# A jump over unused TensorE code, and fifteen tiny loads, in a decode attention kernel

## The chip, the core and the metric

The kernel runs on one core of a Trainium2 chip. A core has five engines with programs of their own: TensorE (PE: matrix products into PSUM; the profile keeps its weight loads apart as PEld), VectorE (DVE), ScalarE (ACT), GpSimd (POOL) and SyncE (SP), which here only issues transfers. [...] Engines wait for each other by semaphores. The metric is the device time of one execution in microseconds; lower is better.

## The reference

One decode step for a batch of two: attention over a cache of 4096 keys with 16 query heads on 8 key-value heads of width 256, gated by a small feed-forward network. All is float32.

```python
xn = layernorm(x)                       # x: (2, 1, 448)
q = xn @ wq                             # 16 heads of 256
p = softmax(q @ k_cache^T * 256**-0.5)  # k_cache, v_cache: (2, 8, 4096, 256)
s = (p @ v_cache) @ wo                  # back to 448
h = (xn @ w_gate) * (xn @ w_up)         # 1792 wide
g = silu(h @ w_down)
out = x + s * g
```

The caches are 134 MB of the 158.5 MB that are read, and each byte is used once.

## The kernel before, in words

`N = 16` units of work, one for each pair of a key-value head and a batch row. A unit needs 4 MB of keys and 4 MB of values. The host lays the data out so that one transfer of 8 MB (`kv[1 + i]`, line 172) brings the keys of unit i+2 beside the values of unit i. Two buffers of 64 KB on each of 128 partitions (`buf[0]`, `buf[1]`) take these transfers in turn; `low` holds the gate, up and later the output weights.

**SyncE's queue** (`dma_side`, lines 160 to 185) sets the order of all large loads: gate and up weights in two pieces (line 163), `wz`, a strip of the up weights, from four rows of HBM to sixteen partitions (line 164), `wd` (165), `wq` (166). Then, each behind a wait for the product that frees its buffer: the first unit's and the second's keys (169), fourteen transfers of 8 MB (172), the last two units' values (175), the output weights in six pieces (180), the result (182). Each load counts 16 on a semaphore when it has landed. ScalarE issues two small loads of x at its start (223, 225).

**TensorE** (`pe_side`, line 358) runs one program in order: transposes of the normalised x; gate and up products (403) once `gu` is full; the feed-forward's down product (409, key "y4") and its sums (412); q's products (415) and their transposes (418, key "qt"). Then for units 0 and 1 `scores`, `highest` and `spread_highest` (lines 463 to 467), with `turn(0)` between, and a loop of `LOOPS = 7` turns (line 471) with two units each: `turn` transposes the exponentials, `scores` is the next keys' product, `values` the product with the values, `join` collects heads. Behind the loop come the last two units and the output weights (495 to 511). `scores` first waits for `q`, which GpSimd counts up when a unit's q is laid out (line 219), and for the keys' load.

`Queue.after` (line 50) makes one engine wait for a numbered point of another's program; `Queue.loop` (line 70) opens a loop on the hardware and passes further arguments on to `nc.Fori`. [...] VectorE and ScalarE run their own loops, with softmax's maxima, exponentials and sums, paced by TensorE.

Of the kernel before, what the change touches and what calls it, by code (L numbers as in the profile page):

```python
# [5 lines left out]
PE = mybir.EngineType.PE  # L6
# [18 lines left out]
EPS = 1e-5  # L25
N = HKV * B
LOOPS = 7
SIDE = 256
GU = (0, 2 * FC, 28 * FC - SIDE)
GROUPS = 4  # L30
# [59 lines left out]
def program(nc, known, x, xo, wgu, wz, wd, wq, kv, vv, wo, out):  # L90
    def flat(w, lo, hi):
        return w[128 * lo:128 * hi].rearrange("(p n) -> p n", p=128)

    def sb(name, shape):
        return nc.alloc_sbuf_tensor(name, shape, F32).ap()

    def ps(name, shape):
        return nc.alloc_psum_tensor(name, shape, F32).ap()

    first = nc.alloc_semaphore("first")  # L100
    sems = {n: nc.alloc_semaphore(n) for n in (
        "x", "xg", "gu", "wd", "wq", "k0", "k1", "v14", "v15", "t0", "t1", "pt", "sr", "ob", "q", "m", "mx", "res")}
    won = [nc.alloc_semaphore(f"wo{i}") for i in range(len(ABREAST + DIRECT))]
    pe = Queue(nc, nc.tensor, "pe", known)
    dv = Queue(nc, nc.vector, "dv", known)
# [15 lines left out]
    xg, gate, sig, r0, r1 = (sb(n, [128, SL]) for n in ("xg", "gate", "sig", "r0", "r1"))  # L121
# [8 lines left out]
    m = sb("m", [128, 2])  # L130
    mx = sb("mx", [1, NT, W])
    p = sb("p", [128, 2, 512])
    su = sb("su", [128, 2])
    sr = sb("sr", [128, 128])
    r = sb("r", [128, N, REP])
    pT = sb("pT", [128, 2, BLK, 128])
    ob = sb("ob", [128, 512])
    oT = sb("oT", [128, REP, 2, N, DUP])

    s = ps("s", [128, 2, 512])  # L140
    sm = ps("sm", [128, 512])
    pt = [ps(f"pt{i}", [128, NK, 128]) for i in range(2)]
# [4 lines left out]
    late = buf[1][:, ROW:]  # L147
    side = late[:4 * GROUPS, :8 * SIDE]
    bounds = [0]
# [10 lines left out]
    def dma_side():  # L160
        e = nc.sync
        for lo, hi in zip(GU, GU[1:]):
            e.dma_start(low[:, lo:hi], flat(wgu, lo, hi)).then_inc(sems["gu"], 16)
        e.dma_start(side, wz[:, :4]).then_inc(sems["gu"], 16)
        e.dma_start(buf[1][:, :14 * D], wd).then_inc(sems["wd"], 16)
        e.dma_start(buf[0][:, :28 * 512], wq).then_inc(sems["wq"], 16)
        sp.after(pe, "y4")
        for h in range(2):
            e.dma_start(buf[1][:, h * ROW:(h + 1) * ROW], kv[0][:, h * ROW:(h + 1) * ROW]).then_inc(sems[f"k{h}"], 16)
        for i in range(N - 2):  # L170
            sp.after(pe, *(("q", 1) if i == 0 else ("s", 1) if i == 1 else ("v", i - 2)))
            e.dma_start(buf[i % 2], kv[1 + i]).then_inc(turns[i % 2], 16)
        sp.after(pe, "v", N - 4)
        for h in range(2):
            e.dma_start(buf[0][:, h * ROW:(h + 1) * ROW], vv[h]).then_inc(sems[f"v{N - 2 + h}"], 16)
        for n, lo, hi in zip(won, bounds, bounds[1:]):
            if lo == early:
                sp.after(pe, "v", N - 3)
            t = low[:, lo * D:hi * D] if hi <= early else late[:, (lo - early) * D:(hi - early) * D]
            e.dma_start(t, flat(wo, lo * D, hi * D), single_packet=True).then_inc(n, 16)  # L180
        sp.after(dv, "res")
        e.dma_start(out, r1).then_inc(sems["res"], 16)
        e.wait_ge(sems["res"], 16)
        last = nc.alloc_semaphore("last")
        e.sem_clear(range(first.num, last.num + 1))

# [171 lines left out]
    def pe_side():  # L358
        e = nc.tensor

        def rows(t, w, n, cut=0):
            def block(i):
                return w[:, i * n:(i + 1) * n - (cut if i == 13 else 0)]
            for k in range(3):
                for c in range(NT):
                    e.matmul(t[W * c:W * (c + 1), :n], xnT[:, k, :], block(NT * k + c), start=k == 0, stop=False)  # L366
            if cut:
                z = side.rearrange("p (a k n) -> p a k n", a=2, k=NK)
                for k in range(NK):
                    for c in (1, 3):  # L370
                        e.matmul(t[W * c:W * (c + 1), n - cut:n], xzT[:, k, :], z[:, c // 2, k, :],
                                 start=False, stop=False)
            for c in range(NT):
                half = slice(0, 64) if c < 2 else slice(64, 128)
                ins = e.matmul(t[W * c:W * (c + 1), :n - cut * (c % 2)], xnT[half, 3, :], block(12 + c % 2)[half],
                               start=False, stop=True)
            return ins
# [24 lines left out]
        for w in range(2):  # L402
            pe.ev(rows(s[:, w], low[:, w * 14 * FC:(w + 1) * 14 * FC], FC, w * SIDE), "gu", w)
        pe.after(dv, "h")
# [15 lines left out]
        def scores(i, k):  # L420
            pe.take(sems["q"])
            k = k.rearrange("p (h d c n) -> p h d c n", h=2, d=2, c=NT)
            for h in range(2):
                for d in range(2):
                    for c in range(NT):
                        ins = e.matmul(s[W * c:W * (c + 1), h], qs[i % 2][:, d].rearrange("p j q -> p (j q)"),  # L426
                                       k[:, h, d, c, :], start=d == 0, stop=d == 1)
            pe.ev(ins, "s", i)

        def highest(i):  # L430
            pe.take(sems["m"])
            pe.ev(e.transpose(sm[:1, :128], m[:, 0:1], ident), "m", i)  # L432

        def spread_highest(i):
            pe.take(sems["mx"])
            pe.ev(e.matmul(sm[:, 128:129], mx.rearrange("p c j -> p (c j)"), one, start=True, stop=True), "x", i)  # L436

        def turn(i):
            pe.take(sems["sr"])
            for h in range(2):  # L440
                pe.ev(turned(pt[h], p[:, h]), "t", i, h)
            pe.ev(e.matmul(sm[:, 130:132], sr, sel[:, 0], start=True, stop=True), "u", i)  # L442

        def values(i, v, between):
            v = v.rearrange("p (h i c n) -> p h i c n", h=2, i=BLK, c=2)
            for h in range(2):
                for j in range(BLK):
                    between.get((h, j), lambda: None)()
                    for c in range(2):
                        at = 2 * (j % 2) + c  # L450
                        ins = e.matmul(o[W * at:W * (at + 1), :], pT[:, h, j, 64 * c + 16:64 * c + 48],  # L451
                                       v[:, h, j, c, :], start=h == 0 and j < 2, stop=h == 1 and j >= 2)
            pe.ev(ins, "v", i)

        def join(i):
            pe.take(sems["ob"])
            for d in range(2):
                for h in range(2):
                    ins = e.matmul(oc[:, 2 * d:2 * d + 2], ob[:, h * 256 + d * 128:h * 256 + (d + 1) * 128], sel[:, h],  # L459
                                   start=h == 0, stop=h == 1)  # L460
            pe.ev(ins, "j", i)

        for i in range(2):
            e.wait_ge(sems[f"k{i}"], 16)
            scores(i, buf[1][:, i * ROW:(i + 1) * ROW])
            highest(i)
            spread_highest(i)
            if i == 0:
                turn(0)

        with pe.loop(nc, PE, LOOPS, head_slot={PE: 0}):
            for i in range(2):
                pe.take(sems["pt"], 2)
                turn(i + 1)
                pe.take(turns[i], 16)
                scores(i + 2, buf[i][:, ROW:])
                values(i, buf[i][:, :ROW], {(0, 3): lambda: highest(i + 2), (1, 2): lambda: spread_highest(i + 2)})
                join(i)
# [35 lines left out]
    act_side()  # L514
    dve_side()
    dma_side()
    pe_side()
    return {q.name: q.at for q in (pe, dv, ac, po, sp)}

# [53 lines left out]
```

## Time and profile before

| | |
|---|---|
| device time, median of 3 runs | 374.89 us (374.56 to 375.03) |
| device time of the profiled execution | 374.87 us |
| its span in the profile | 373.1 us |
| bytes moved, mean rate over the span | 158.68 MB, 425 GB/s |
| TensorE matmul busy, mean granted clock | 247.5 us (66%), 0.799 |
| VectorE, ScalarE, GpSimd busy | 58.4 us, 46.5 us, 5.9 us |

The page gives for each engine its busy time; a strip of digits for forty equal slices of the span (9 means 90% or more); the DMA queues with their packets, MB and share of the time of all sixteen DMA engines; and the chain of work that ended last. Queue q1 is SyncE's, q10 ScalarE's, q8 carries blocks of TensorE's program. A view by stretches cuts the span at chosen times and gives for each stretch the length, the busy time and number of instructions of each engine, the granted clock, the share of the sixteen DMA engines that was busy, and GB/s. The view of the DMA queues can be cut to a stretch as well; its shares then are of sixteen engines over that stretch.

### The profile page before, as it was taken

How to read it: one execution, taken by the hardware profiler on the slowest of the kernel's cores; microseconds unless marked ns; L12 is line 12 of the kernel's file. 1: busy time of each engine (PE TensorE's matmuls, PEld its weight loads, DVE VectorE, ACT ScalarE, POOL GpSimd, SP SyncE). 2: the span in 40 equal slices, each digit the busy share in tenths (PEclk: the TensorE clock that was granted, in tenths of full speed). 3: DMA queues.
4: the chain of work that ended last, by engine and by line, in shares of the span. 5: the costliest groups of instructions: out<-in, count | busy, mean ns of one | idle time of the engine just before them, and what ended most of it. 6: DMA issues, size and time to landing. Idle time of an engine off the chain costs nothing. (4 is left out here: it accounts for less than half of the span.)

```text
span 373.1 us, 3992 instructions
## 1 busy us (share of the span) xinstructions
PE 247.5 (66%) x1662; PEld 100.2 (27%) x1662; DVE 58.4 (16%) x132; ACT 46.5 (12%) x111; POOL 5.9 (2%) x30
## 2 busy tenths in 40 slices
PE   0097485539393949585767767576857585948785
PEld 0022123122223232323232314132222323232432
DVE  3001003202121212121120212030303020202100
ACT  1000231200201020202020202020202020112100
POOL 2000000000000000000000000000000000000000
PEclk9996699858786776877685968595969595869899
DMA  9999999999999999999999999999999999999995
GB/s 363 407 460 450 405 436 425 451 444 422 436 444 429 414 450 443 414 436 450 429 414 450 443 414 436 450 429 414 450 443 414 436 443 422 429 422 436 415 418 229
DMA packets 4221, 158.68 MB, mean 425 GB/s; under 512 B 614, under 2 KB 872, under 8 KB 1256
## 3 DMA queue, kind: packets, MB, share of 16 engines
q1 hardware_dynamic: 4196, 158.59, 98.6%
q8 instruction: 5, 0.08, 0.1%
q10 hardware_dynamic: 20, 0.01, 0.0%
HBM read 158.54 MB, written 0.06 MB: 425 GB/s over the span
## 5 line engine op out<-in xcount | busy, mean ns | idle before, releaser
L426 PE MATMUL s<-buf,qs 128*32 128x512 f32 x512 | 85.9, 831 | 53.2 <-PEq L87 53.2
L451 PE MATMUL o<-buf,pT 128*32 128x512 f32 x512 | 76.0, 602 | 0.3 <-DVE oT L328 0.3
L246 ACT ACTIVATE p<-s,m 128x512 f32<-128x512 f32 x32 | 21.7, 682 | 250.7 <-DVE m L310 250.7
L426 PEld LDWEIGHTS s<-buf,qs 128*32 128x32 f32 x512 | 21.8, 147 | 104.2 <-issue 104.2
L304 DVE TENSOR_REDUCE m<-s 128x1 f32<-128x1024 f32 x16 | 19.6, 1225 | 167.8 <-PE s L426 167.8
L381 PE MATMUL pt<-ident,p 128*128 128x128 f32 x128 | 26.1, 372 | 17.9 <-PEq L87 17.9
L459 PE MATMUL oc<-sel,ob 128*128 128x2 f32 x128 | 16.4, 250 | 19.8 <-PEq L87 19.8
L381 PEld LDWEIGHTS pt<-ident,p 128*128 128x128 f32 x128 | 20.4, 188 | 18.8 <-issue 18.8
L451 PEld LDWEIGHTS o<-buf,pT 128*32 128x32 f32 x512 | 16.9, 110 | 31.5 <-issue 29.1
L459 PEld LDWEIGHTS oc<-sel,ob 128*128 128x128 f32 x128 | 15.5, 191 | 33.9 <-issue 33.9
L366 PE MATMUL s<-low,xnT 128*32 128x448 f32 x48 | 6.9, 725 | 12.4 <-DMA buf<-wz 12.4
L323 DVE COPY pT<-pt 128x512 f32<-128x512 f32 x16 | 11.1, 692 | 19.6 <-PE o L451 18.5
L306 DVE TENSOR_REDUCE mx<-sm 1x128 f32<-1x512 f32 x16 | 10.9, 679 | 10.1 <-PE sm L432 10.1
L258 ACT COPY ob<-o 128x512 f32<-128x512 f32 x16 | 9.3, 582 | 12.6 <-PE o L451 12.6
L366 PE MATMUL s<-buf,xnT 128*32 128x512 f32 x48 | 7.1, 737 | 4.9 <-DMA buf<-wq 4.9
L251 ACT COPY pT<-pt 128x512 f32<-128x512 f32 x16 | 9.6, 601 | 2.3 <-PE pt L381 2.3
L328 DVE TENSOR_TENSOR oT<-oc,r 128x64 f32 (+1 forms) x16 | 3.6, 225 | 32.5 <-PE oc L459 32.5
L442 PEld LDWEIGHTS sm<-sel,sr 128*128 128x128 f32 x32 | 8.6, 330 | 0.0
L436 PEld LDWEIGHTS sm<-one,mx 1*128 1x128 f32 x32 | 4.7, 183 | 13.8 <-issue 13.8
L219 POOL COPY qs<-qT 128x64 f32<-128x64 f32 x16 | 3.7, 237 | 292.6 <-PE s L426 243.1
L386 PE MATMUL o<-low,oT 128*32 128x448 f32 x54 | 6.4, 544 | 1.2 <-DMA low<-wo 1.2
L436 PE MATMUL sm<-one,mx 1*128 1x1 f32 x32 | 6.0, 254 | 1.7 <-PEq L87 1.7
(70 smaller groups left out, 73.6 us busy)
## 6 DMA issues: line engine op xcount, KB each, us to landing
buf<-kv SPq DMA_DIRECT2D x2, 4096.0 KB, 20.3
buf<-vv SPq DMA_DIRECT2D x2, 4096.0 KB, 22.2
buf<-wq SPq DMA_DIRECT2D x1, 7168.0 KB, 40.2
low<-wgu SPq DMA_DIRECT2D x1, 5696.0 KB
buf<-wd SPq DMA_DIRECT2D x1, 3136.0 KB, 23.5
low<-wo SPq DMA_DIRECT2D x1, 3136.0 KB, 33.9
low<-wo SPq DMA_DIRECT2D x1, 2016.0 KB, 38.2
low<-wo SPq DMA_DIRECT2D x1, 896.0 KB, 39.9
```

The source lines that it names most:

```text
L246: ins = e.activation(p[:, h], s[:, h], AF.Exp, bias=m[:, 1:2], scale=1.0 / 16, accum_out=su[:, h:h + 1])
L251: e.copy(pT[:, 1], pt[1]).then_inc(sems["pt"], 1)
L258: e.copy(ob, o).then_inc(sems["ob"], 1)
L304: e.tensor_reduce(m[:, 0:1], s.rearrange("p h n -> p (h n)"), axis=AX.X, op=OP.max).then_inc(sems["m"], 1)
L306: e.tensor_reduce(mx, sm[:1, None, :128].rearrange("p o (c j) -> p o j c", c=NT).to_broadcast([1, NT, W, NT]), axis=AX.X, op=OP.max).then_ ...
L323: e.tensor_copy(pT[:, 0], pt[0]).then_inc(sems["pt"], 1)
L366: e.matmul(t[W * c:W * (c + 1), :n], xnT[:, k, :], block(NT * k + c), start=k == 0, stop=False)
L381: ins = e.transpose(t[:, i, :], a[:, i * 128:(i + 1) * 128], ident)
L426: ins = e.matmul(s[W * c:W * (c + 1), h], qs[i % 2][:, d].rearrange("p j q -> p (j q)"), k[:, h, d, c, :], start=d == 0, stop=d == 1)
L436: pe.ev(e.matmul(sm[:, 128:129], mx.rearrange("p c j -> p (c j)"), one, start=True, stop=True), "x", i)
L451: ins = e.matmul(o[W * at:W * (at + 1), :], pT[:, h, j, 64 * c + 16:64 * c + 48], v[:, h, j, c, :], start=h == 0 and j < 2, stop=h == 1 an ...
L459: ins = e.matmul(oc[:, 2 * d:2 * d + 2], ob[:, h * 256 + d * 128:h * 256 + (d + 1) * 128], sel[:, h], start=h == 0, stop=h == 1)
```

## The change

Three things change. SyncE gets fifteen loads between `wd` and `wq`: the load of k rows (k = 1 to 15) brings k rows of 16 numbers of x, 64 bytes a row, to k partitions of a new tensor `lab`. Nothing reads `lab`; at the end SyncE waits for all fifteen. TensorE gets, behind q's transposes, a register that holds 0 and a branch on it: the code that would run if it weren't 0 is 1,720 waits, and it is always passed over. And TensorE's loop loses its `head_slot`.

```diff
+FILL = 1720
...
-        "x", "xg", "gu", "wd", "wq", "k0", "k1", "v14", "v15", "t0", "t1", "pt", "sr", "ob", "q", "m", "mx", "res")}
+        "x", "xg", "gu", "wd", "wq", "k0", "k1", "v14", "v15", "t0", "t1", "pt", "sr", "ob", "q", "m", "mx", "lab", "res")}
...
+    lab = sb("lab", [16, 240])
+    xr = x.rearrange("b (k n) -> (b k) n", n=16)
...
         e.dma_start(buf[1][:, :14 * D], wd).then_inc(sems["wd"], 16)
+        for k in range(1, 16):
+            e.dma_start(lab[:k, (k - 1) * 16:k * 16], xr[:k]).then_inc(sems["lab"], 16)
         e.dma_start(buf[0][:, :28 * 512], wq).then_inc(sems["wq"], 16)
...
         e.wait_ge(sems["res"], 16)
+        e.wait_ge(sems["lab"], 15 * 16)
...
+        never = e.alloc_register("never")
+        e.reg_mov(never, 0)
+        with e.If_ne(never, 0):
+            for _ in range(FILL):
+                e.wait_ge(sems["gu"], 16)
+
         for i in range(2):
             e.wait_ge(sems[f"k{i}"], 16)
             scores(i, buf[1][:, i * ROW:(i + 1) * ROW])
...
-        with pe.loop(nc, PE, LOOPS, head_slot={PE: 0}):
+        with pe.loop(nc, PE, LOOPS):
```

The change's own description says that TensorE's program "jumps to its sixth block".

## The prediction

> **What bounds the kernel now.** I read the strip of forty slices first, then the table of DMA queues, then the chain that ended last.
>
> ```profile
> PE   0097485539393949585767767576857585948785
> DMA  9999999999999999999999999999999999999995
> DMA packets 4221, 158.68 MB, mean 425 GB/s; under 512 B 614, under 2 KB 872, under 8 KB 1256
> q1 hardware_dynamic: 4196, 158.59, 98.6%
> q8 instruction: 5, 0.08, 0.1%
> DMA 7%; PE 3%; DVE 0%; issue 0%
> ```
>
> The 16 DMA engines are busy in every slice; SyncE's queue alone (q1) fills 98.6% of their time. TensorE idles between loads. The chain is short because it starts at the last weight loads, which had been queued long before. The span is the time in which 16 engines move 158.68 MB, and as all feed every transfer, the end is that of the engine with the most to carry. So I ask of each edit which DMA engine it loads. The second queue that matters is q8: five packets of 0.08 MB in all, 16 KB each, TensorE's own program.
>
> ```profile
> core 0: us, PE busy (x) PEld busy (x) DVE busy (x) ACT busy (x) POOL busy (x), PEclk, DMA share, GB/s
> 368.00:368.20 0.20, 0.20 (x8) 0.00 (x0) 0.00 (x0) 0.00 (x0) 0.00 (x0) 1.00 0.96 367
> 368.20:368.60 0.40, 0.40 (x7) 0.00 (x0) 0.00 (x0) 0.00 (x0) 0.00 (x0) 1.00 0.71 269
> 368.60:369.30 0.70, 0.04 (x1) 0.00 (x0) 0.00 (x0) 0.53 (x1) 0.00 (x0) 1.00 0.58 220
> 369.70:369.90 0.20, 0.20 (x16) 0.20 (x12) 0.00 (x0) 0.00 (x0) 0.00 (x0) 1.00 0.14 54
> 369.90:370.10 0.20, 0.20 (x18) 0.20 (x13) 0.00 (x0) 0.00 (x0) 0.00 (x0) 1.00 0.01 0
> buf<-wz SPq DMA_DIRECT2D x1, 128.0 KB
> ```
>
> These stretches show the engines running dry. The share is 0.96 until 368.2, falls to 0.58 by 368.6, stays there, and is gone at 369.9. A share of 0.58 is 9.3 engines: seven stop between 368.0 and 368.6, nine go on to between 369.3 and 369.9. I read the nine as five with one program block each and four with `wz`. `wz` is loaded from 4 rows, so I put its 128 KB on four engines: 32 KB at 425 / 16 = 26.6 GB/s, 1.2 us each. 4 + 5 = 9 fits only if no engine carries both; one that did would have run on past 370.4.
>
> **The program blocks.**
>
> ```profile
> 0.00:35.10 35.10, 15.12 (x108) 5.04 (x112) 4.35 (x13) 2.23 (x4) 2.23 (x14) 0.92 0.98 418
> 35.10:67.70 32.60, 21.54 (x157) 7.45 (x153) 3.88 (x11) 6.94 (x15) 0.65 (x3) 0.82 0.98 425
> 67.70:77.50 9.80, 4.88 (x33) 2.84 (x25) 2.36 (x4) 1.45 (x4) 0.24 (x1) 0.82 1.04 450
> 77.50:106.40 28.90, 18.24 (x117) 6.71 (x121) 3.29 (x7) 2.41 (x6) 0.24 (x1) 0.71 0.99 429
> DMA packets 2099, 108.34 MB, mean 432 GB/s; under 512 B 232, under 2 KB 232, under 8 KB 232
> q1 hardware_dynamic: 2099, 108.34, 99.8%
> ```
>
> I cut the stretches at the fetches (35.1, 67.7, 77.6, 106.5, 359.2). The x behind PEld counts weight loads, each with a matmul. By the code 280 pairs stand ahead of the loop, 170 in its body, 192 behind: 280 + 7 x 170 + 192 = 1662, the page's count. The third fetch comes 290 pairs in, ten after the loop's head; the fourth after 131 pairs of the loop, some 270 instructions with its waits. [...] The last two lines are q1 alone from 108 to 359 us: no q8 line, so six back edges fetch nothing.
>
> **The change part by part.**
>
> *The jump.* [...]
>
> ```profile
> PE s L426 <- PEq L87: 6.3, 2, 5.4
> 82.42 1.94 PE L426 MATMUL s<-buf,qs 128*32 128x512 f32 x8 [5.38 <-PEq L87]
> q8 instruction: 1, 0.02, 3.1%
> q8 instruction: 1, 0.02, 3.4%
> 69.87 0.33 SPq L172 DMA_DIRECT2D buf<-kv  x1
> ```
>
> TensorE must wait at the target for block six. The trace of before shows no such wait. Its least is one fetch, 3.1% of 16 engines in two us = 0.99 us (3.4% = 1.09 in the slowest); its most, with two 64 KB packets of 2.4 us ahead on that engine (65,536 B at 26.6 GB/s), 6 us. I take 3. Queued behind it are scores(0), turn(0), scores(1), and SyncE's load of the second block of keys, issued at 69.87 when scores(1) ends. The cover: TensorE sits idle 5.38 us ahead of the scores at 82.42, waiting for a load that ends there, and the queue is full until then, 12 us after 69.87. So the stall costs nothing; six us would pass 0.6 into a loop with 53 us of such idle time. The compare and the register move lie under the same cover.
>
> [...]
>
> *What the blocks do to DMA engines.* A block costs its engine from 0.62 us (16 KB at 26.6 GB/s) to 1.6 us (369.9 less 368.3, the middle of the plain engines' ends). I take 1.3, between the packet's own 1.0 and the 1.6. [...] A plain engine with one block ends where such engines end now. A `wz` engine with a block ends at 369.5 + 1.3.
>
> *Fifteen loads.* [...]
>
> ```profile
> q10 hardware_dynamic: 8, 0.00, 1.8%
> q10 hardware_dynamic: 8, 0.00, 0.6%
> 3.18 0.51 SPq L166 DMA_DIRECT2D buf<-wq  x1
> 1.65 0.79 SPq L164 DMA_DIRECT2D buf<-wz  x1
> buf<-wd SPq DMA_DIRECT2D x1, 3136.0 KB, 23.5
> 371.48 0.35 SPq L182 DMA_DIRECT2D res<-r  x1
> ```
>
> The nearest rows are the eight 448-byte rows of `xg` (1.8% of 16 engines in 0.7 us, 25 ns each) and their eight semaphore writes (0.6%, 8 ns). [...] I take 0.4 on `wz`'s engines. Alone this is hidden: 369.5 + 0.4 is 369.9, the end as it is. On SyncE the loads stand ahead of `wq`, at 0.35 to 0.79 us an issue: `wq`, issued at 3.18 now, goes out between 8.4 and 15.0. `wd` ahead of it lands at about 2.5 + 23.5 = 26, so the queue stays full, and the next issue waits for y4 at 37. The wait at the end is met long before; under 0.1 us.
>
> [...]
>
> **The sum.** The profiled execution took 374.87 us, with a span of 373.1 and 1.8 around it; the runs' median is 374.89. Jump 0, issue 0, small loads 0 by themselves. With block eight, nine or ten on one of `wz`'s engines: 369.5 + 1.3 + 0.4 = 371.2 against 369.9, **+1.3 us, 376.2**. Its ends: 369.3 + 0.6 + 0.1 is 370.0 (+0.1), 369.9 + 1.6 + 0.5 is 372.0 (+2.1); by the prices that I hold likely 375.6 to 376.8. The slip carries to the end in full, as the last products wait for the last weights:
>
> ```profile
> 344.08 25.18 DMA buf<-wo
> 369.30 0.78 PE acc L504 x24
> ```
>
> **The rivals.**
>
> *Not slower: the new blocks miss `wz`'s engines.* [...] From -0.1 to +0.5 us; I take +0.2, **375.1**. For it: five fetches of before all missed. It turns into the forecast once one of two or three blocks meets one of four engines. If engines are given evenly among the eleven left, two blocks miss with 7/11 x 6/10 = 0.38, three with 0.21. [...]
>
> [...]
>
> *The change doesn't do what it says:* the fill is laid elsewhere, or the same engines carry as many blocks. Then the small loads alone, 0 to +0.3, **375.0**.
>
> *Faster* by more than 0.2%: four engines of `wz` end no sooner than 369.3, 0.6 us ahead of now, whatever the blocks do. Hardly.
>
> **How the numbers follow.** Forecast 0.56; miss 0.32; blocks don't stay 0.05; not as said 0.07. About 0.2%, 0.75 us, is what a measurement here can tell. Slower by more: 0.52 of the forecast's 0.56 (the rest ends under +0.75), 0.05, and 0.02 of a miss: 0.59. Faster 0.03, from a miss with cheaper engines than I think. Same 0.38. The range runs from 374.6 (a miss, less 0.2 and the runs' spread) to 377.0 (+2.1); it leaves out the store that loses blocks and the far tails. The likeliest case alone: 375.6 to 376.8.
>
> **What would show it.** q8 with five or six packets: one at 35 as now, two close together at 52 to 60, one in the loop's first turns, none later, one or two near 358. TensorE's first scores later than 54.73 by 1 to 6 us, those at 82.42 unmoved. In the last two us one or two engines still running from 370.1 to 371.3, where before had none: this decides between forecast and miss. I am wrong if the share falls to zero by 370.2; if the tail is long for many engines, the small loads cost more than 33 ns; if q8 has 20 packets, blocks don't stay.

## The result and the profile after

The changed kernel takes 377.28 us (median of 5 runs, 376.26 to 377.58) against 374.81 for the kernel before in the same comparison (374.56 to 375.03): ratio 1.0058, interval 1.0040 to 1.0077. That is 2.47 us more. The forecast was 376.2 in a range of 374.6 to 377.0: slower was right, the size was too small by half and the median lies 0.28 us above the range. The profiled execution took 377.52 us with a span of 376.0.

First the strip of GB/s on the page of the kernel before, and then, from the page of the changed kernel, the same strip, the packets, and the program's queue.

```profile
GB/s 363 407 460 450 405 436 425 451 444 422 436 444 429 414 450 443 414 436 450 429 414 450 443 414 436 450 429 414 450 443 414 436 443 422 429 422 436 415 418 229
```

```profile
GB/s 360 404 409 417 418 436 448 441 376 434 446 446 432 439 418 404 439 446 432 446 441 432 439 418 418 432 446 425 446 446 432 439 418 411 439 425 422 423 421 213
DMA packets 4462, 158.70 MB, mean 422 GB/s; under 512 B 854, under 2 KB 1112, under 8 KB 1496
q8 instruction: 6, 0.10, 0.1%
```

241 packets more than the 4221 of before: 1 + 2 + ... + 15 = 120 rows of 64 bytes, as many semaphore writes, and one program block more. The page agrees: 240 packets more under 512 B (854 against 614), so the rows of these fifteen loads took one packet of data and one semaphore write each. Two places of the strip are low against the kernel before: the third and fourth slice (19 to 38 us, 409 and 417 against 460 and 450) and the ninth (75 to 85 us, 376 against 444). The stretches around them, in the kernel before and then in the changed one:

```profile
22.00:32.00 10.00, 8.22 (x68) 2.51 (x60) 1.31 (x3) 0.79 (x3) 0.00 (x0) 0.88 1.06 460
72.00:96.00 24.00, 14.75 (x87) 6.35 (x87) 3.44 (x7) 3.85 (x10) 0.24 (x1) 0.72 1.01 435
```

```profile
22.00:32.00 10.00, 8.53 (x68) 2.56 (x60) 1.30 (x3) 0.53 (x1) 0.00 (x0) 0.92 1.03 415
72.00:96.00 24.00, 17.39 (x109) 7.65 (x111) 5.47 (x10) 3.48 (x9) 0.47 (x2) 0.73 0.97 413
```

In the first stretch the engines move 415 instead of 460 GB/s: the fifteen loads pass there, with their 64-byte packets from 24.3 to 26.9 us. In the second their share is 0.97 instead of 1.01. A share has to be read with care: a packet is counted in the stretch in which it begins, with all of its time, so a share can pass 1, and one round of sixteen packets of 2.4 us is 0.2 of a stretch of 12 us. Over the 12 us that the expectations below name (78 to 90 us) the shares are 0.92 and 1.01, and the ten kernels that show no hole scatter there from 0.96 to 1.02; over 72 to 96 us they lie between 0.99 and 1.01. Added up from the packets' starts and durations in the traces, sixteen packets are under way at every time from 74 to 92 us in the kernel before, and only about nine at 81 to 82 us in the changed one. That is the hole. What stands around that hole shows in the timeline of the changed kernel, TensorE's lines first and then SyncE's:

```profile
55.37 1.43 PE L387 MATMUL pt<-ident,qr 128*128 128x128 f32 x8
62.91 6.08 PE L432 MATMUL s<-buf,qs 128*32 128x512 f32 x32 [6.11 <-PEq L88]
76.34 4.49 PE L432 MATMUL s<-buf,qs 128*32 128x512 f32 x32
87.99 5.48 PE L432 MATMUL s<-buf,qs 128*32 128x512 f32 x32
8.48 0.39 SPq L171 DMA_DIRECT2D buf<-wq  x1
80.90 0.33 SPq L177 DMA_DIRECT2D buf<-kv  x1
```

q's transposes begin at 55.37 (52.37 before). The jump then leaves TensorE idle for 6.11 us. scores(0) takes 6.08 us instead of 3.64, at a granted clock of 0.59 instead of 1.00, as the stretch of these products shows in the kernel before and in the changed one:

```profile
54.70:58.40 3.70, 3.64 (x32) 1.12 (x32) 0.00 (x0) 0.81 (x1) 0.06 (x1) 1.00 1.03 443
```

```profile
62.90:69.00 6.10, 6.08 (x32) 1.49 (x32) 0.00 (x0) 0.00 (x0) 0.00 (x0) 0.59 1.11 475
```

SyncE's second transfer of 8 MB, which waits for scores(1), is issued at 80.90 instead of 69.87. (The expectations below call it the third unit's keys; "the keys" in what follows is this transfer; by line 172 of the kernel before it brings the fourth unit's keys and the second unit's values.) It is 11.03 us late: 3.00 of late start, 5.18 of stall (62.91 less 54.73, less those 3.00), 2.44 of slow scores, 0.4 of the rest. By then the engines that were ahead had moved all that was queued: of sixteen, ten are at work at 81.0 us and nine from 81.3 to 82.0.

The end of the changed kernel answers to the tail shown in the prediction:

```profile
370.40:370.80 0.40, 0.40 (x5) 0.16 (x8) 0.00 (x0) 0.00 (x0) 0.00 (x0) 1.00 1.00 376
370.80:371.20 0.40, 0.40 (x8) 0.00 (x0) 0.00 (x0) 0.00 (x0) 0.00 (x0) 1.00 0.71 264
371.20:371.60 0.40, 0.28 (x4) 0.00 (x0) 0.00 (x0) 0.05 (x1) 0.00 (x0) 1.00 0.43 166
372.40:372.80 0.40, 0.40 (x28) 0.40 (x24) 0.00 (x0) 0.00 (x0) 0.00 (x0) 1.00 0.11 40
372.80:373.20 0.40, 0.40 (x24) 0.29 (x14) 0.00 (x0) 0.00 (x0) 0.00 (x0) 1.00 0.00 0
```

All sixteen engines run until 370.8, not until 368.2, and the last stops at about 372.8, not at 369.9. The first to stop slipped by 2.6 us and the last by 2.9. One or two engines that met a program block would have left the first at 368.2: the loss reached every engine of this execution.

### The profile page after: what moved, and what is told of

Read it like the earlier page. It is cut to its first block, busy times and chain, and to the rows that moved or that the text cites. A ratio compares the mean times of both kernels' runs of the same rounds, so it can differ in the third digit from the quotient of the medians.

```text
span 376.0 us, 4009 instructions
## 1 busy us (share of the span) xinstructions
PE 253.9 (68%) x1662; PEld 102.4 (27%) x1662; DVE 58.4 (16%) x132; ACT 46.6 (12%) x111; POOL 6.0 (2%) x30
## 5 line engine op out<-in xcount | busy, mean ns | idle before, releaser
L432 PE MATMUL s<-buf,qs 128*32 128x512 f32 x512 | 91.0, 873 | 49.2 <-PEq L88 49.2
L432 PEld LDWEIGHTS s<-buf,qs 128*32 128x32 f32 x512 | 24.4, 153 | 102.4 <-issue 102.1
L372 PE MATMUL s<-buf,xnT 128*32 128x512 f32 x48 | 8.1, 828 | 6.3 <-DMA buf<-wq 6.3
```

## The experiments

Each was compared with the kernel before on the same chip. Ratios are to the kernel before, with their intervals; its median was 375.02 us for the first four, 374.97 for the next four and 374.9 for the last two.

**The fifteen loads alone.** The change without the jump and with `head_slot` kept; the tensor `lab` and the wait at the end, not printed here, are as in the change:

```diff
         e.dma_start(buf[1][:, :14 * D], wd).then_inc(sems["wd"], 16)
+        for k in range(1, 16):
+            e.dma_start(lab[:k, (k - 1) * 16:k * 16], xr[:k]).then_inc(sems["lab"], 16)
         e.dma_start(buf[0][:, :28 * 512], wq).then_inc(sems["wq"], 16)
```

> Theory A: the small loads, not a meeting of a program block with the wz engines, make the larger part of the loss. In the changed kernel wq lands at 8.48 + 36.8 = 45.3 us against 3.18 + 40.2 = 43.4 before, so the slowest engine is 1.9 us late before any new block has been fetched. Then the loads alone cost +1.4 to +2.2 us (376.2 to 377.0), wq lands at 45 or later, five fetches on q8, and no dip of the DMA share at 78 to 90 us. Theory B, the forecast as it was recorded (a new block on one of wz's engines, loads at 33 ns each): 0 to +0.3 us, wq lands by 43.9.

376.40 us, ratio 1.0034 (1.0022 to 1.0046): +1.4 us. wq lands at 8.50 + 37.4 = 45.9. The stretches of this kernel show the first low group without the second:

```profile
22.00:32.00 10.00, 8.32 (x68) 2.51 (x60) 1.31 (x3) 0.70 (x2) 0.00 (x0) 0.88 0.97 409
78.00:90.00 12.00, 7.20 (x46) 3.69 (x50) 0.24 (x1) 0.00 (x0) 0.00 (x0) 0.60 1.00 433
```

The loads make more than half of the loss by themselves, with five program blocks as before. Theory A holds for them. The end of this kernel's profiled execution (377.20 us, one of the slowest two of six):

```profile
368.20:368.60 0.40, 0.40 (x8) 0.13 (x4) 0.00 (x0) 0.00 (x0) 0.00 (x0) 1.00 0.99 390
368.60:369.00 0.40, 0.40 (x8) 0.13 (x4) 0.00 (x0) 0.00 (x0) 0.00 (x0) 1.00 0.72 291
372.00:372.40 0.40, 0.40 (x24) 0.40 (x20) 0.00 (x0) 0.00 (x0) 0.00 (x0) 1.00 0.07 27
372.40:372.80 0.40, 0.40 (x27) 0.35 (x16) 0.00 (x0) 0.00 (x0) 0.00 (x0) 1.00 0.00 0
```

Here the first engines stop at about 368.6, some 0.5 us later than in the kernel before, and the last at 372.4, 2.5 us later: this fits loads of 1 to 15 rows that fall on the engines unequally; no trace names a packet's engine. In the change the ends are 370.8 and 372.8. So between these two executions the first engines lost 2.2 us more, and the last, whose end is the kernel's, only 0.4 us: this fits a hole that falls on the engines that were ahead.

**The jump alone**, without the fifteen loads:

```diff
+        never = e.alloc_register("never")
+        e.reg_mov(never, 0)
+        with e.If_ne(never, 0):
+            for _ in range(FILL):
+                e.wait_ge(sems["gu"], 16)
...
-        with pe.loop(nc, PE, LOOPS, head_slot={PE: 0}):
+        with pe.loop(nc, PE, LOOPS):
```

> Jump over 1,720 waits and no head_slot, without the fifteen loads. Theory A: the stall at the branch is there (3 to 7 us), but q's products end 2 to 3 us sooner than with the loads, so the load of the third unit's keys is issued at 77 to 79 us instead of 80.9 and the queue doesn't run dry, or hardly: -0.2 to +0.6 us (374.6 to 375.4). Theory B: a new block meets one of wz's engines, +0.9 to +1.4 us (375.7 to 376.2). Theory C, the stall alone dries the queue: the DMA share of 78 to 90 us falls to 0.95 or less and the time rises by 0.5 us or more without any meeting.

375.77 us, ratio 1.0017 (1.0006 to 1.0029), in a spread from 374.33 to 376.64. The median lies above the range of A (374.6 to 375.4) and just inside that of B (375.7 to 376.2), so by the time alone B looks better; the spread covers both. The profiled execution is the fastest, 374.33 us: a stall of 5.97 us, keys issued at 76.44, no hole (share 1.01 from 78 to 90 us). The slower executions left no profile, so theory C is neither seen nor excluded here.

**No `head_slot`**, nothing else:

```diff
-        with pe.loop(nc, PE, LOOPS, head_slot={PE: 0}):
+        with pe.loop(nc, PE, LOOPS):
```

> The loop without its head_slot, nothing else. [...] All theories: 4 or 5 fetches, none in the loop's later turns, -0.4 to +0.2 us. If the time moves by more than 0.5 us, the place of the loop in its blocks matters by itself.

374.80 us, ratio 0.9995 (0.9987 to 1.0004), five blocks on q8. What `head_slot` does to the loop's place in the program the traces don't show; leaving it out is worth nothing that can be measured here.

**The changed kernel with the jump ahead of q's products**, where TensorE waits for wq anyway, and gone from its old place:

```diff
+        never = e.alloc_register("never")
+        e.reg_mov(never, 0)
+        with e.If_ne(never, 0):
+            for _ in range(FILL):
+                e.wait_ge(sems["gu"], 16)
+
         e.wait_ge(sems["wq"], 16)
         for h in range(2):
             pe.ev(rows(s[:, h], buf[0][:, h * 14 * 512:(h + 1) * 14 * 512], 512), "q", h)
```

> The changed kernel with the jump moved ahead of q's products, where TensorE waits for wq's load anyway (6.3 us there in the changed kernel). Theory A with C: the stall is covered there, scores(0) starts at 57 to 59 us instead of 62.9, the third unit's keys are issued at 70 to 75 us, the DMA share of 78 to 90 us is back at 1.0, and the time is the loads' alone: 376.1 to 376.9, 0.5 to 1.2 us below the changed kernel. Theory B: one fetch more, time as the changed kernel's, 377 to 378.

376.39 us, ratio 1.0035 (1.0022 to 1.0048), against 1.0058 for the change; the intervals just overlap. It is the time of the loads alone. In this kernel's timeline scores(0) starts at 58.22 and the keys go out at 74.15:

```profile
58.22 2.35 PE L438 MATMUL s<-buf,qs 128*32 128x512 f32 x20 [0.94 <-PEq L88]
74.15 0.33 SPq L177 DMA_DIRECT2D buf<-kv  x1
```

The hole is gone from its stretches (share 1.02), though its program's queue has seven blocks and the change's six:

```profile
78.00:90.00 12.00, 8.07 (x46) 3.80 (x50) 0.29 (x1) 0.69 (x3) 0.00 (x0) 0.57 1.02 438
```

```profile
q8 instruction: 7, 0.11, 0.1%
```

**The loads alone, each of 16 rows:**

```diff
-            e.dma_start(lab[:k, (k - 1) * 16:k * 16], xr[:k]).then_inc(sems["lab"], 16)
+            e.dma_start(lab[:, (k - 1) * 16:k * 16], xr[:16]).then_inc(sems["lab"], 16)
```

> The fifteen loads alone, each of 16 rows instead of 1 to 15 (240 rows for 120). Theory A2: a small load in SyncE's queue costs each engine that it uses some 0.15 us of idle time, whatever its bytes (120 rows took wq's landing from 43.4 to 45.3 us and 0.02 of the DMA share of 22 to 32 us). Then all engines pay 15 times, none is spared: wq lands at 45.3 to 46.2, and the time is as with the loads alone or above, +1.6 to +2.6 us (376.6 to 377.6). Theory D: what costs is that the engines are loaded unequally; with equal loads the time falls back to +0.2 to +0.7 us (375.2 to 375.7).

376.98 us, ratio 1.0058 (1.0045 to 1.0071): +2.0 us, and wq lands at 45.6 (issued at 10.35, 35.2 to landing). The time doesn't fall back, it rather rises (the intervals just meet). Now the whole end moves: the engines are full until 370.0, 1.8 us later than in the kernel before, and the last stops at about 372.1, 2.2 us later. The first and the last are late nearly alike, so unequal loading isn't the cause (theory D falls).

```profile
369.60:370.00 0.40, 0.40 (x8) 0.13 (x8) 0.00 (x0) 0.00 (x0) 0.00 (x0) 1.00 1.03 403
371.60:372.00 0.40, 0.40 (x20) 0.40 (x24) 0.00 (x0) 0.00 (x0) 0.00 (x0) 1.00 0.27 103
372.00:372.40 0.40, 0.40 (x26) 0.40 (x20) 0.00 (x0) 0.00 (x0) 0.00 (x0) 1.00 0.02 5
```

2.0 us for fifteen loads is 0.13 us each, some four times the 33 ns (25 and 8) of the prediction.

**The loads alone, from ScalarE's queue**, with `lab` and the wait at the end as in the change:

```diff
         e.dma_start(xg[0:128:DUP, :], xo).then_inc(sems["xg"], 16)
+        for k in range(1, 16):
+            e.dma_start(lab[:k, (k - 1) * 16:k * 16], xr[:k]).then_inc(sems["lab"], 16)
```

> The fifteen loads alone, of 1 to 15 rows as in the change, but issued by ScalarE behind xg's load, so that they lie in another queue beside the large weights. Theory A2: a DMA engine has another queue's packets to move while a small load's round trip lasts; what is left is 33 ns a row, 0.5 us on the first engine: 0 to +0.6 us (375.0 to 375.6), wq lands by 44. Theory E: each small load costs its engine the same in any queue: +1.2 to +1.8 us, as the loads alone in SyncE's queue.

375.60 us, ratio 1.0019 (1.0011 to 1.0028): +0.6 us, wq at 3.21 + 40.7 = 43.9. The same rows cost less than half from ScalarE's queue, +0.6 for +1.4 us. The interval overlaps that of the loads alone a little (1.0022 to 1.0046), but two more pairs that differ in the loads' queue alone fall the same way: 1.0035 and 1.0016 with the jump ahead of q, 1.0058 and 1.0034 with the jump as in the change. The stretch of this kernel that holds wq's first packets is nearly as full as before; below it stands ScalarE's queue in the same stretch:

```profile
22.00:32.00 10.00, 8.26 (x76) 2.49 (x68) 1.31 (x3) 0.74 (x3) 0.00 (x0) 1.00 1.04 447
```

```profile
q10 hardware_dynamic: 62, 0.00, 0.4%
```

0.4% of sixteen engines over 10 us for 62 packets is 10 ns a packet, 20 ns for a row with its semaphore write. In the change, from SyncE's queue, a 64-byte packet takes 8 to 11 ns and a semaphore write 9. So the packets' own time doesn't make the 0.13 us a load in SyncE's queue. That an engine there waits out each tiny load before it goes on is how I read it; the traces don't show the wait itself. In the changed kernel only nine to twelve packets are under way from 24.8 to 26.5 us, where the kernel before has sixteen, so engines do idle there. In the changed kernel with the jump ahead of q fifteen or sixteen are, and the same stretch shows a high share at fewer GB/s than before, engines on record as busy that move less:

```profile
22.00:32.00 10.00, 8.85 (x72) 2.49 (x64) 0.98 (x3) 0.53 (x1) 0.00 (x0) 0.95 1.11 443
```

**The jump alone, ahead of q's products**, without the loads; its edits are those of the jump alone and of the moved jump.

> The jump without the fifteen loads, moved ahead of q's products. Theory A with C: the stall of 6.4 us lies beside the wait for wq (4.9 us there), the third unit's keys are issued by 72 to 74 us, the queue never runs dry, and the time is that of before, -0.4 to +0.4 us (374.6 to 375.4) with a spread of less than 1 us. Theory B, blocks on engines that have something else to carry: +0.5 to +1.2 us, since the same blocks and one more are fetched.

375.00 us, ratio 0.9999 (0.9986 to 1.0011), 374.77 to 375.48. The timeline of this kernel, TensorE's first product behind the jump and SyncE's issue of the keys, and then its program's queue:

```profile
44.05 5.35 PE L367 MATMUL s<-buf,xnT 128*32 128x512 f32 x24 [6.50 <-DMA buf<-wq]
72.17 0.33 SPq L173 DMA_DIRECT2D buf<-kv  x1
```

```profile
q8 instruction: 7, 0.11, 0.1%
```

The same 1,720 waits lie ahead of the code behind q's transposes as in the change. Seven blocks are fetched, one more than in the change, and the time is that of before. This speaks against theory B, and with it against the forecast's mechanism: no block of these seven met an engine at which it cost anything. The traces don't name a block's engine, so that each block met the same engine as in the change isn't shown; there it is the tail that speaks against it, in which every engine is late.

**Two jumps in a row**, over 860 waits ahead of q's transposes and over 1,720 behind them, no loads:

```diff
+        def jump(n):
+            with e.If_ne(never, 0):
+                for _ in range(n):
+                    e.wait_ge(sems["gu"], 16)
+
+        jump(FILL // 2)
         for h in range(2):
             pe.after(ac, "qr", h)
             pe.ev(turned(pt[h], qr[h]), "qt", h)
...
+        jump(FILL)
         for i in range(2):
             e.wait_ge(sems[f"k{i}"], 16)
```

> No loads; two jumps, one ahead of q's transposes over 860 waits and one behind them over 1,720, so two stalls of some 6 us in a row. Theory C: the third unit's keys are issued at 82 to 84 us, 2 to 4 us past the time when the engines have moved all that was queued (about 80 to 82 us), the DMA share of 78 to 90 us falls to 0.75 to 0.85, and the time rises by what the queue was empty, +2 to +4.5 us (377 to 379.5). Theory B: two more fetches and no more than that, 0 to +1.2 us.

385.44 us, ratio 1.0253 (1.0228 to 1.0278): +10.5 us, more than twice what I expected, because three stalls came instead of two. The timeline of this kernel, TensorE's lines and SyncE's, and then one of its stretches:

```profile
56.11 1.11 PE L382 MATMUL pt<-ident,qr 128*128 128x128 f32 x8 [3.64 <-issue]
64.46 3.30 PE L436 MATMUL s<-buf,qs 128*32 128x512 f32 x14 [7.24 <-PEq L88]
72.73 5.13 PE L436 MATMUL s<-buf,qs 128*32 128x512 f32 x18 [4.97 <-issue]
90.05 0.33 SPq L173 DMA_DIRECT2D buf<-kv  x1
```

```profile
80.00:90.00 10.00, 7.43 (x44) 3.54 (x44) 1.57 (x5) 2.03 (x5) 0.00 (x0) 0.66 0.04 15
```

The third stall, 4.97 us, lies inside scores(0), after 14 of its 32 products. A block's packet begins in it, between 70.3 and 70.4, and takes 1.0 us (62.6% of sixteen engines over 0.1 us), and the products go on 1.3 us after its end. That TensorE waited for this block is how I read it; the timeline names no releaser there:

```profile
q8 instruction: 1, 0.02, 62.6%
```

The keys go out at 90.05, and from 80 to 90 us almost nothing begins: a share of 0.04, 9.6 us lost against 10.5 measured. Three fetches more than the jump alone (nine packets on q8 against six), at 1.0 us for a packet, can't cost that. This shows directly how a stall of TensorE becomes time.

**Both edits kept, both moved:** the loads to ScalarE, the jump ahead of q's products.

> The changed kernel with both edits kept but moved: the fifteen loads issued by ScalarE, the jump ahead of q's products. If the loss of the change is the round trips of the loads in SyncE's queue (theory A2) and the late issue of the third unit's keys behind the stall (theory C), and nothing else, what is left is what the loads cost in the other queue: +0.3 to +0.9 us (375.2 to 375.9), third unit's keys issued by 75 us, DMA share of 78 to 90 us at 1.0. If seven program blocks on engines that carry wz or small loads count (theory B): +1.2 us or more.

375.60 us, ratio 1.0016 (1.0004 to 1.0028): +0.7 us, keys issued at 72.24, share 0.99. What is left is what the loads cost in ScalarE's queue.

**The loads moved, the jump where the change has it:**

> The changed kernel with the loads issued by ScalarE and the jump where the change has it. Theories A2 and C: the loads' +0.6 and the jump's +0.7 alone add up, +0.8 to +1.9 us (375.8 to 376.9), with a spread of 1 us and more, since the issue of the third unit's keys falls at 77 to 80 us, close to the time when the queue runs dry; in a profiled execution above 376.3 the DMA share of 78 to 90 us is below 0.98.

375.99 us, ratio 1.0034 (1.0022 to 1.0045), 375.52 to 377.25: +1.1 us. Keys issued at 77.26. The share is 0.96 from 78 to 90 us, but 1.01 from 72 to 96 us, and by the packets' starts and durations sixteen are under way at every time from 74 to 92 us: no hole. The profiled execution was the fastest, 375.52 us, so what was expected of one above 376.3 wasn't seen. The interval overlaps that of the kernel before this one.

Ordered by the time at which the keys are issued, the profiled executions are:

| kernel | keys issued, us | DMA share, 72 to 96 us | profiled time, us |
|---|---|---|---|
| before | 69.87 | 1.01 | 374.87 |
| no `head_slot` | 70.20 | 1.00 | 374.78 |
| loads alone, of 16 rows | 72.00 | 1.01 | 377.04 |
| jump alone, ahead of q | 72.17 | 0.99 | 374.96 |
| both moved | 72.24 | 1.01 | 375.90 |
| loads alone, ScalarE's queue | 72.67 | 1.00 | 375.51 |
| loads alone | 73.38 | 1.01 | 377.20 |
| changed, jump ahead of q | 74.15 | 1.01 | 376.39 |
| jump alone | 76.44 | 1.00 | 374.33 |
| loads moved | 77.26 | 1.01 | 375.52 |
| changed | 80.90 | 0.97 | 377.52 |
| two jumps | 90.05 | 0.55 | 386.33 |

A hole is there at 80.90 and larger at 90.05, and there is none up to 77.26. The times differ among the upper rows by what the loads cost, which this column doesn't tell.

Three pairs differ in the place of the jump alone: 1.0058 and 1.0035 (the change), 1.0034 and 1.0016 (loads moved), 1.0017 and 0.9999 (no loads). In each the two intervals overlap a little, but all three put the jump behind q's transposes 0.7 to 0.9 us above the jump ahead of q's products. Only the change's profile shows a hole with it; the other two profiled executions were the fastest of their kernels.

## Why the prediction came out as it did

**What bounds the kernel** was read rightly: the DMA engines, and the slowest of them. The hole is a time in which engines had nothing to move: about nine packets under way for sixteen at 81 to 82 us. What the loads cost is less clear: engines idle in some executions and are on record as busy, moving less, in another.

**The forecast's mechanism was wrong.** The step that failed is "With block eight, nine or ten on one of `wz`'s engines". The jump alone ahead of q's products fetches seven blocks and costs nothing (0.9999), and the change's tail has every engine late, not one or two. What the prediction called a miss fits the blocks. No run shows which blocks of the program were fetched, or on which engines they and the small loads fell: block eight, nine or ten on one of `wz`'s engines, and the 0.4 us (0.1 and 0.5 at the ends of the range) that those engines pay for small loads, were my estimates. The runs show six packets on q8 in the change, seven without loss with the jump alone ahead of q's products, and +1.4 us for the loads in SyncE's queue. That the direction came out right is luck: it has two other reasons, worth 1.4 and about 1 us, which the sum had put at 0.4 and at nothing.

**Fifteen loads: a term mis-sized.** The 33 ns a row were the durations of `xg`'s packets and semaphore writes, which had come through ScalarE's queue, with SyncE's packets to move beside them. From that queue the whole costs +0.6 us, near the 0.4 of the sum. In SyncE's own queue it is 0.13 us a load by the loads of 16 rows, +1.4 us in all for those of 1 to 15. "Alone this is hidden" failed with it. The issue itself was costed rightly: fifteen in 5.24 us, wq issued at 8.48, inside 8.4 to 15.0, and no harm by that.

**The stall: "So the stall costs nothing" failed.** The stall was 6.1 us, just past my bound of 6, and I had taken 3. The cover of 12 us behind 69.87 was the right one to look at, but three things came out of it together: the late start that the loads cause (3.00 us), the stall (5.18 us net) and the slower scores behind it (2.44 us). I had counted one. And the cover ends sooner than the landing at 82.42 on which I put it: that is when the last engine is done, and an issue at 80.90 came too late for those that were ahead. In the change it costs about 0.9 us (1.0058 less 1.0035 with the jump moved, of 375; the intervals just overlap); that a late issue costs time is shown by the two jumps.

**The blocks.** Five or six were forecast, six came; the pair that I expected close together at 52 to 60 us began at 60.3 and 66.4. The loop refetches nothing turn by turn: q8 brings one packet between 92 and 366 us, and six in all, not the 20 by which blocks that don't stay were to show. Dropping `head_slot` cost nothing (0.9995); the sum has no term for it.

**What would show it.** TensorE's first scores came 8.2 us late, not 1 to 6, and those at 82.42, which I expected unmoved, begin at 87.99: both signs failed. The sign for the forecast was one or two engines running on past 370.1. The tail showed all sixteen until 370.8, close to the sign that I gave for dearer small loads, "if the tail is long for many engines".

**The spread.** The change's runs lie in two groups, 376.26 and 376.33, and 377.28 to 377.58. It is tempting to give the lower no hole, but only the upper group left a profile, and the loads alone fall into the same two groups (376.10 to 376.55, and 377.20 and 377.25), with no hole in the profiled 377.20. What parts the groups is open.

## What to carry to other kernels

This kernel, bound by DMA, paid for edits of a few bytes and no work at all. A row of tiny loads between two large ones in the same queue cost about 0.13 us each, several times their packets' own time of 20 ns a row; from the other queue such loads cost less than half, +0.6 for +1.4 us. A stall of an engine that looks idle must be followed to the next large load that waits for it, and added to every other delay on that path, before it is called covered.

## What the hardware showed that was not expected

- The jump over 1,720 waits left TensorE idle for about 6 us (6.11 in the change, 5.97 for the jump alone, 5.53 with the loads moved). In the change the sixteen DMA engines were full beside it, with a share of 1.01 from 56.8 to 62.9 us. There q's transposes end at 56.80, a block's packet begins between 60.2 and 60.4 and takes 0.9 us, and scores(0) begins at 62.91. So some 3.5 us pass before the packet begins and 1.7 us behind its end; why, the trace doesn't show.
- Behind the stall the granted clock was 0.59 for the next 6 us, where the kernel before had 1.00 at the same products. That made 2.44 us of the delay. The same products took 5.45 us behind the stall of the jump alone and 5.80 us with the loads moved, at 0.66 and 0.62, and 3.64 us in every kernel without a stall right ahead of them.
- The last block that comes during the loop doesn't come at a fixed time. In the changed kernel's queues, cut at 92 to 192, 192 to 196 and 196 to 366 us, it comes once, in the loop's third turn:

```profile
q1 hardware_dynamic: 747, 43.71, 101.0%
q1 hardware_dynamic: 21, 1.38, 80.2%
q8 instruction: 1, 0.02, 1.6%
q1 hardware_dynamic: 1598, 73.33, 99.8%
```

With the loads moved and the same jump it comes at 117 to 118 us, in the first turn, and with the jump alone at 232 to 233 us, in the fourth. What sets the time isn't shown.
